# Two one-bank PSUM tiles in place of one two-bank tile, and a new hand-written order

## The chip, the cores and the metric

The kernel runs on one core of a Trainium2 chip. The time is device microseconds from launch to finish. TensorE does the matrix products, VectorE (DVE) and ScalarE (ACT) move and transform tiles, GpSimd (POOL) does a few memsets, and SyncE (SP) issues every DMA. Matrix products land in PSUM, which has eight banks of 128 partitions by 512 fp32 numbers.

## The reference, cut to what matters

```python
# x: 4 batches of 12480 tokens of 128 channels; inducing: 32 x 128
def mab(q, kv):
    a = softmax(q @ kv.T / sqrt(128))
    return a @ kv
h   = mab(inducing, x)          # 32 rows per batch, a sum over all tokens
y   = mab(x, h)                 # every token against the 32 rows
hid = y @ w_in                  # 128 -> 2048
out = (hid - tanh(hid)) @ w_out # 2048 -> 128
```

## The kernel before

**Tiling.** A batch of 12480 tokens is cut into seven slices of 1792 tokens (the last one overlaps its neighbour by 64). A slice of x, channels on partitions, is 896 KB (0.9175 MB) and takes one of 19 places called `big`; all 28 slices are loaded once. The pairs of slices (0,1), (2,3), (4,5) and (6) share one score tile each.

**First pass, for each batch b.** I call the steps by short names. `ldx s` loads slice s. `S1.s` (L275) makes the scores of a slice against the inducing rows, eight matmul records. `max1.g` (L299, DVE) moves the scores of pair g out of PSUM and takes a maximum. `spread1`, `fold1` (L313), `nb1` (L315) turn the maxima into one number. `exp1.g` (L324, ACT) and `tr1.g` (L326, DVE) give weights with tokens on partitions. The same slice is also needed with tokens on partitions: either `LDXN s` loads it a second time from a transposed copy in HBM, or `turn s.h` (L345, seven TensorE transposes for each half h) and `cpy s.h` (a copy of 128x896 by ACT, L168, or DVE, L170) make it. The set `LOADED` says which slices are loaded twice. `ACC s` (L357) adds the slice to the 32 sums over tokens in PSUM. `foldsum` (L365), `recip` (L369), `whole` (L375 or L377), `hT` (L379) and `cphT` end the batch's sum.

**Between the passes.** A small chain puts the 32 rows through the two weight matrices in linearised form: `up` (L275 with win_sb), `turned`, `tanh`, `series`, `tangent`, `column` (L435), `cpP1`, `points` (L441, L442), `cpP4`, `cpPm`, `away`, `far`. The weights arrive as 64-bit numbers and are put together as fp32 by DVE and ACT, five DVE steps and two ACT steps for each of eight blocks (L237 to L258).

**Second pass.** `S2.s`, `max2.g` (L478), `spread2`, `ones2` (L487), `nb2` (L490), `wg`, `exp2.g` (L500), then `L s` (L514): eight matmul records into two PSUM tiles, emptied by `ev s.0` and `ev s.1` (L530 on ACT or L532 on DVE), and `st s` stores the slice from its `big` place. The last two slices of the last batch are stored in halves, as soon as each half is emptied. A final chain (`bpe`, `bcopy`, `pick`, `least`, `bturn`, `gather`, `decide`) writes one flag that decides whether a general, slow path runs; with these inputs it does not.

**Order.** `ORDER` is a written list. Each word is the number of a step, the engine (P, A, D, S, G) and letters that choose places in the pools for its new tiles. Each engine runs its steps in this order, and so does SP: a DMA that waits holds up all DMAs behind it. Waits are made from the order: a step waits for those earlier in the list that touch the same tile, if one of them writes it.

**PSUM.** Three tiles `d` of two banks each take scores, transposes and outputs (six banks). One more tile of two banks, `side`, holds the rest: its first bank is the place `s` (the sums over tokens, `up`, `pick`, `bturn`), its second bank has three places `q` for all the small products. Two output halves, those in `SIDE`, batch 3 slice 0 half 1 and batch 3 slice 3 half 0, are written into the whole of `side` instead of a `d` tile.

Of the kernel before, what the change touches and what calls it, by code (L numbers as in the profile page):

```python
# [10 lines left out]
F32 = mybir.dt.float32  # L11
# [25 lines left out]
SIDE = frozenset(((3, 0, 1), (3, 3, 0),))  # L37
LOADED = frozenset(((0, 5), (1, 3), (1, 4), (1, 6), (2, 3), (2, 5), (2, 6), (3, 1), (3, 2), (3, 4), (3, 5), (3, 6),))
# [17 lines left out]
277Ac 372P 376Db 461Pgb 380A 278A 374P 473Sm 459P 301Pack 462D 381P 466Peb 302A 385Da 386Sd 390D 196S 464P 303A 292Pcas 293A 467D 383P 317A 471Phb
469P 294D 295S 472D 296Pacf 318A 298A 297D 327A 387P 304S 474Pcb 391Ab 475D 319Pacd 321D 482Pbl 392Pa 320A 299S 477D 483A 484Pa 393D 485A 323Pbcs
478Pa 154D 408Pda 322S 324A 325D 487Sk 407P 479D 409D 480A 197Pcba 326S 394Pa 410Pba 481Da 411P 395Db 198A 199A 396A 328Pbch 502Sj 412D 329A 486Pa
330A 398D 399Dc 436Pia 435P 437D 179Pcbr 476G 491Sf 489A 488P 500Sd 413Da 498A 506Si 504A 508D 400Pa 495Pak 181D 414Pc 415D 180A 509Pb 496A 490Da 397A
200S 493Pc 494A 401Aa 305Pabs 405Dc 182S 307D 510D 499Db 492P 402Pa 417A 306D 416A 403Aa 497P 404A 418Pbcf 501P 438Pha 331S 439D 505Da 426A 419A 503P  # L60
420A 427Pcbn 406D 440Dc 429D 507P 441Pa 511Ab 512Pb 428A 442D 431Pbar 513D 444A 432A 421S 514Pa 443A 527Pbc 433D 449Pbah 515Dc 453A 528P 451A 518D
529D 516A 519Db 517A 430S 450A 434S 530Pca 531P 308S 452S 581A 532D 454Pbco 456A 455A 525Da 520Pb 533Db 521Ac 457S 526D 445Pacq 446A 534Pa 535D 522Pb
524D 447A 448S 422Pbar 523Ac 555Pic 537A 582D 424D 423A 556P 557D 538Pahabac 542Pbcp 536A 546A 539A 540D 425S 541S 543D 558Pda 559D 580D 544A
551Pboaabc 583Ac 560Da 547Pacq 552A 553D 561Pa 562D 584Am 585Pa 564A 548A 549D 563A 565Pbcr 566D 586Aa 587Pa 574A 575Pabh 545S 567A 554S 550S 9Pc 578A
576A 588Da 589Pa 569Pbco 568S 570A 579S 577S 590D 571S 591D 7Pa 572D 573S 8Pa 5Pa
# [47 lines left out]
def fused_kernel(ctx, tc, xT, xn, indT, w_in, w_out, outT):  # L113
# [21 lines left out]
    pspool = ps_scope.__enter__()  # L135
# [36 lines left out]
    def place(tag):  # L172
        return Buf(lambda b: slots[tag][b.slot], tag)
# [7 lines left out]
    def fixed(t):  # L181
        return Buf(lambda b: t)
# [276 lines left out]
    def second(b, P4, Pm):  # L459
        def group(G):  # L460
# [34 lines left out]
            for g in G:  # L495
# [6 lines left out]
                def last(j, s):  # L502
                    ot, ds, outs, whole = place("big"), [], [], [[], []]
# [245 lines left out]
```

## Time and profile before

| | us |
|---|---|
| median of 3 runs | 178.69 |
| the three runs | 177.58, 178.69, 178.9 |
| the profiled execution | 177.38 |
| its span, first to last instruction | 175.6 |

The profiled execution is one run of its own; its span leaves out 1.78 us of its time. TensorE is busy for 149.2 us of the span, DVE for 126.7 and ACT for 110.8, and DMA packets fill 94.6% of the 16 DMA engines' time. No engine is busy all the time, so a busy share alone does not say which one sets the end. The table of stretches and the lists of waits do.

### The profile page before, as it was taken

How to read it: one execution, taken by the hardware profiler on the slowest of the kernel's cores; microseconds unless marked ns; L12 is line 12 of the kernel's file. 1: busy time of each engine (PE TensorE's matmuls, PEld its weight loads, DVE VectorE, ACT ScalarE, POOL GpSimd, SP SyncE). 2: the span in 40 equal slices, each digit the busy share in tenths (PEclk: the TensorE clock that was granted, in tenths of full speed). 3: DMA queues.
4: the chain of work that ended last, by engine and by line, in shares of the span. 5: the costliest groups of instructions: out<-in, count | busy, mean ns of one | idle time of the engine just before them, and what ended most of it. 6: DMA issues, size and time to landing. Idle time of an engine off the chain costs nothing.

```text
span 175.6 us, 4692 instructions
## 1 busy us (share of the span) xinstructions
PE 149.2 (85%) x1946; PEld 86.3 (49%) x1946; DVE 126.7 (72%) x290; ACT 110.8 (63%) x166; POOL 1.2 (1%) x10
## 2 busy tenths in 40 slices
PE   0779959999999899899977999999969898998900
PEld 0644628763376755535766545436656424434400
DVE  4285957899999949399782457698783798797810
ACT  2376419953568767485378456869737687999800
POOL 1000000000000000000000000000000000000000
PEclk9999999999999999999999999999999999999985
DMA  5999999999999999999999989999997698999991
GB/s 190 413 412 420 418 410 419 400 419 419 421 417 415 420 418 371 280 412 328 400 423 425 405 353 411 371 324 420 425 423 329 253 410 368 412 394 410 413 392 63
DMA packets 11405, 66.85 MB, mean 381 GB/s; under 512 B 1392, under 2 KB 1392, under 8 KB 11376
## 3 DMA queue, kind: packets, MB, share of 16 engines
q1 hardware_dynamic: 11376, 66.47, 94.6%
q8 instruction: 17, 0.28, 0.6%
q14 instruction: 12, 0.10, 0.2%
HBM read 40.91 MB, written 25.56 MB: 379 GB/s over the span
## 4 chain that ended last, share of the span: by engine, by line
PE 47%; DMA 19%; DVE 16%; ACT 9%; issue 4%; SPq 1%; ACTq 0%; DVEq 0%
PE d L275 12%; PE d L514 12%; PE side L357 10%; DMA big<-in_xT 9%; DMA big<-in_w_out 6%; PE d L345 5%; DMA big<-in_w_in 4%; DVE big L532 3%; ACT big L530 3%; ACT sl L324 2%; DVE sl L478 2%; PE side L435 2%; PE side L487 2%; DVE sl L299 2%; DVE et L326 1%
## 5 line engine op out<-in xcount | busy, mean ns | idle before, releaser
L530 ACT ACTIVATE big<-d,Pm,wg 128x896 f32<-128x896 f32 x35 | 37.4, 1093 | 14.1 <-PE d L514 11.2
L168 ACT COPY big<-d 128x896 f32<-128x896 f32 x29 | 25.6, 910 | 22.6 <-PE d L345 22.5
L345 PE MATMUL d<-ident,big 128*128 128x128 f32 x224 | 30.8, 285 | 7.6 <-DMA big<-in_xT 6.6
L345 PEld LDWEIGHTS d<-ident,big 128*128 128x128 f32 x224 | 25.9, 148 | 15.1 <-issue 7.2
L357 PE MATMUL side<-big,et 128*32 128x128 f32 x784 | 28.3, 275 | 3.4 <-DVE rs L369 1.4
L357 PEld LDWEIGHTS side<-big,et 128*32 128x32 f32 x784 | 23.1, 110 | 14.9 <-issue 6.2
L514 PE MATMUL d<-sl,k 32*128 32x448 f32 x216 | 29.6, 584 | 0.2
L275 PE MATMUL d<-big,indT_sb 128*32 128x448 f32 x224 | 27.1, 544 | 2.3 <-DMA big<-in_xT 2.1
L532 DVE TENSOR_SCALAR big<-d,wg,Pm 128x896 f32<-128x896 f32 x19 | 22.9, 1203 | 3.6 <-PE d L514 2.0
L275 PE MATMUL d<-big,hT 128*32 128x448 f32 x224 | 24.7, 543 | 0.5 <-ACT big L530 0.4
L299 DVE TENSOR_SCALAR_CACHE_REDUCE sl<-d 128x896 f32<-128x896 f32 (+1 forms) x16 | 15.5, 970 | 11.6 <-PE d L275 11.5
L478 DVE TENSOR_SCALAR_CACHE_REDUCE sl<-d 128x896 f32<-128x896 f32 (+1 forms) x16 | 15.4, 968 | 4.5 <-PE d L275 4.5
L500 ACT ACTIVATE sl<-sl,nbs 128x896 f32<-128x896 f32 (+1 forms) x16 | 15.2, 947 | 4.5 <-DVE nbs L490 4.5
L326 DVE STREAM_TRANSPOSE et<-sl 128x896 f32<-128x896 f32 (+1 forms) x16 | 15.7, 987 | 0.5 <-ACT sl L324 0.5
L514 PEld LDWEIGHTS d<-sl,k 32*128 32x128 f32 x216 | 9.8, 183 | 12.3 <-issue 4.8
L324 ACT ACTIVATE sl<-sl,nb 128x896 f32<-128x896 f32 (+1 forms) x16 | 15.0, 943 | 0.3 <-DVE nb L315 0.3
L275 PEld LDWEIGHTS d<-big,hT 128*32 128x32 f32 x224 | 7.0, 109 | 13.4 <-issue 7.9
L275 PEld LDWEIGHTS d<-big,indT_sb 128*32 128x32 f32 x224 | 7.5, 109 | 9.1 <-issue 5.0
L490 DVE TENSOR_REDUCE nbs<-side 128x1 f32<-128x128 f32 x8 | 2.3, 289 | 5.7 <-PE side L365 2.4
L244 ACT ACTIVATE big<-big 128x512 f32<-128x512 uint32 x8 | 5.6, 700 | 0.6 <-DMA big<-in_w_out 0.6
L251 DVE SCALAR_TENSOR_TENSOR big<-big 128x512 uint32<-128x512 uint32 x8 | 5.4, 686 | 0.5 <-ACT big L247 0.5
L247 ACT ACTIVATE big<-big,shift 128x512 uint32<-128x512 uint32 x8 | 5.5, 712 | 0.0
(115 smaller groups left out, 126.0 us busy)
## 6 DMA issues: line engine op xcount, KB each, us to landing
big<-in_xT SPq DMA_DIRECT2D x28, 896.0 KB, 11.2
outT<-big SPq DMA_DIRECT2D x23, 896.0 KB, 6.2
big<-in_xn SPq DMA_DIRECT2D x12, 896.0 KB, 12.3
outT<-big SPq DMA_DIRECT2D x3, 864.0 KB, 4.8
big<-in_w_in SPq DMA_DIRECT2D x4, 512.0 KB, 7.3
big<-in_w_out SPq DMA_DIRECT2D x4, 512.0 KB, 13.0
outT<-big SPq DMA_DIRECT2D x3, 448.0 KB, 6.3
outT<-big SPq DMA_DIRECT2D x1, 416.0 KB, 5.7
```

What stands on the lines that cost most here:

```text
L168: nc.scalar.copy(out=out, in_=in_)
L275: nc.tensor.matmul(ps[q * m:(q + 1) * m, :n], lhsT=w, rhs=row, start=True, stop=True)
L299: nc.vector.tensor_scalar(out=sl.get()[:, :n, :], in0=ps.get()[:, :n, :W], scalar1=1.0, scalar2=None, op0=ALU.mult, op1=ALU.max, accum_out ...
L324: nc.scalar.activation(out=t, in_=t, func=AF.Exp, scale=SC, bias=nb.get(), accum_out=sums.get()[:, g:g + 1])
L326: add("DVE", lambda e, et=et, sl=sl, n=len(pair): nc.vector.transpose(out=et.get()[:, :n * KB, :].rearrange("p k i -> p (k i)"), in_=sl.ge ...
L345: nc.tensor.transpose(out=o[:, k * 128:(k + 1) * 128], in_=x.get()[:, at:at + 128], identity=ident)
L357: nc.tensor.matmul(hacc.get()[q * m:(q + 1) * m, :C], lhsT=et.get()[:, j * KB + k, :], rhs=xn_t.get()[:, k * C:(k + 1) * C], start=at < NQ ...
L478: nc.vector.tensor_scalar(out=sl.get()[:, :n, :], in0=ps.get()[:, :n, :W], scalar1=1.0, scalar2=None, op0=ALU.mult, op1=ALU.max, accum_out ...
L500: nc.scalar.activation(out=t, in_=t, func=AF.Exp, scale=SC, bias=nb)
L514: nc.tensor.matmul(ds[q // 2].get()[:, q % 2, :W], lhsT=P4.get()[r, :], rhs=sl.get()[r, j, :], start=True, stop=True)
L530: nc.scalar.activation(out=dst, in_=src, func=AF.Identity, scale=wg.get(), bias=Pm.get())
L532: nc.vector.tensor_scalar(out=dst, in0=src, scalar1=wg.get(), scalar2=Pm.get(), op0=ALU.mult, op1=ALU.add)
```

## The change

The tile `side` becomes two tiles of one bank, `bank_s` and `bank_q`. The three `q` places stay in one bank together, at columns 0, 170 and 340. `SIDE` is gone, so all output halves use `d` tiles. `LOADED` has eleven slices in place of twelve, and others: batch 0 none (before: 5), batch 1 slices 3, 4 (before 3, 4, 6), batch 2 slices 1, 4, 5, 6 (before 3, 5, 6), batch 3 slices 0 to 4 (before 1, 2, 4, 5, 6). `ORDER` is new from the first word to the last.

```diff
-SIDE = frozenset(((3, 0, 1), (3, 3, 0),))
-LOADED = frozenset(((0, 5), (1, 3), (1, 4), (1, 6), (2, 3), (2, 5), (2, 6), (3, 1), (3, 2), (3, 4), (3, 5), (3, 6),))
+LOADED = frozenset(((1, 3), (1, 4), (2, 1), (2, 4), (2, 5), (2, 6), (3, 0), (3, 1), (3, 2), (3, 3), (3, 4),))
...
-    side = pspool.tile([128, 2, 512], F32, name="side")
     slots = {}
     for tag, n in PLACES.items():
         if tag in "sq":
-            slots[tag] = [side[:, 0, :]] if tag == "s" else [side[:, 1, k * 170:(k + 1) * 170] for k in range(n)]
+            bank = pspool.tile([128, 512], F32, name=f"bank_{tag}")
+            slots[tag] = [bank[:, k * 170:] for k in range(n)]
             continue
...
-                    ot, ds, outs, whole = place("big"), [], [], [[], []]
-                    for h in range(2):
-                        if (b, s, h) in SIDE:
-                            ds.append(fixed(side))
-                            whole[h] = [place(tag) for tag in "sqqq"]
-                        else:
-                            ds.append(place("d"))
+                    ot, ds, outs = place("big"), [place("d"), place("d")], []
...
-                    add("PE", pe, reads=[sl, part[g], P4], writes=ds, hold=[ot, *whole[0], *whole[1]])
+                    add("PE", pe, reads=[sl, part[g], P4], writes=ds, hold=[ot])
...
-                        add("ACT/DVE", ev, reads=[ds[h], ot, wg, Pm], writes=[done], hold=whole[h])
+                        add("ACT/DVE", ev, reads=[ds[h], ot, wg, Pm], writes=[done])
```

The two orders, with the numbers replaced by the names of the steps, for the parts that matter below (win and wout are the weight blocks):

```
SP, before, start: b0 ldx1, win3, win0, b0 ldx3, indT, win2, b0 ldx0, ldx2, ldx5, ldx4, ldx6, wout2, b1 ldx1, ...
SP, after,  start: b0 ldx2, wout3, b0 ldx1, indT, b0 ldx0, win3, b0 ldx3, ldx4, ldx5, ldx6, win2, win0, b1 ldx1, ...
SP, before, from the last load: b3 LDXN6, b0 st5, st3, b1 st6, b2 st0, st2, st3, b1 st3, b2 st5, st6, st4, st1,
    b3 st0, st1, st3, st2, st4, st6.1, st6.0, st5.0, st5.1
SP, after,  from the last load: b3 LDXN4, b0 st3, st4, st5, b1 st3, st2, b2 st2, st0, st5, st3, st4, st6, st1,
    b3 st0, st2, st3, st6.0, st6.1, st5.0, st5.1, st1, st4
stores ahead of the last load: 10 before, 9 after
TensorE, before: ... b3 foldsum, turn3.0, b1 L3, b3 ACC2, b2 points, b3 ACC3, b2 L0, b3 ACC4, ...
TensorE, before, the rest of the chain in batch 3: b3 ACC6, b2 ones2.2, b3 hT, b2 L3, b3 up, S2.0, b2 L5, b3 S2.1, S2.2, S2.3,
    b2 L6, b3 column, b2 L4, b3 ones2.0, points, b2 L1, b3 S2.4, S2.5, L0, L1, S2.6, L3, L2, ones2.2, bpe, L4, pick, L6, bturn, L5
TensorE, after, the same part: b3 ACC6, hT, b2 L3, b3 up, S2.0, b2 L5, b3 S2.1, S2.3, S2.2, b2 L4, b3 column, b2 L6,
    b3 points, ones2.0, b2 L1, b3 S2.4, S2.5, L0, S2.6, L2, ones2.2, L3, bpe, L6, pick, L5, bturn, L1, L4
DVE, before, after b0's first maximum: nb1, wout2 (2 steps), tr1.0; b3: recip, tr1.2, b1 ev3.0, b2 max2.3, b3 tr1.3
DVE, after,  after b0's first maximum: nb1, win2 (3 steps), tr1.0; b3: tr1.3, recip; end: least, gather, b3 ev1.0, decide, ev4.0
slices turned by TensorE in batches 0 to 3: 6, 4, 4, 2 before; 7, 5, 3, 2 after
128x896 copies: DVE 3 and ACT 29 before; DVE 8 and ACT 26 after.  Evictions: DVE 20 and ACT 36 before; DVE 19 and ACT 37 after
```

Six small matmuls (`idle0` to `idle5`, L220) keep TensorE going in gaps; both orders have them, in other places.

## Rows read from the trace of the kernel before

**Rows 1.** The page's head, busy time by engine, and DMA totals; the queue's share last.

```profile
span 175.6 us, 4692 instructions
PE 149.2 (85%) x1946; PEld 86.3 (49%) x1946; DVE 126.7 (72%) x290; ACT 110.8 (63%) x166; POOL 1.2 (1%) x10
...
DMA packets 11405, 66.85 MB, mean 381 GB/s; under 512 B 1392, under 2 KB 1392, under 8 KB 11376
...
q1 hardware_dynamic: 11376, 66.47, 94.6%
```

**Rows 2.** Busy us (and instructions) by engine in six stretches; clock, DMA share, GB/s last.

```profile
5.67:24.04 18.37, 15.24 (x114) 9.57 (x114) 13.20 (x23) 9.77 (x13) 0.00 (x0) 1.00 1.02 416
24.04:60.30 36.26, 34.57 (x526) 22.41 (x526) 32.91 (x77) 23.99 (x42) 0.24 (x2) 1.00 1.02 416
60.30:137.05 76.75, 71.69 (x1059) 42.50 (x1059) 53.21 (x114) 49.31 (x75) 0.24 (x2) 1.00 0.98 384
130.00:140.00 10.00, 9.19 (x160) 5.62 (x162) 5.13 (x11) 5.84 (x9) 0.00 (x0) 1.00 0.74 304
137.05:167.60 30.55, 27.71 (x251) 11.76 (x250) 25.45 (x63) 26.43 (x36) 0.00 (x0) 1.00 0.93 379
167.60:175.60 8.00, 0.00 (x0) 0.00 (x0) 0.00 (x0) 0.00 (x0) 0.00 (x0) 0.62 0.57 213
```

**Rows 3.** Timeline: the last first-batch load arrives; first sum over tokens (start, length, ...).

```profile
24.04 0.96 PE L275 MATMUL d<-big,indT_sb 128*32 128x448 f32 x8 [1.68 <-DMA big<-in_xT]
...
29.41 3.24 PE L357 MATMUL side<-big,et 128*32 128x128 f32 x112
```

**Rows 4.** Groups by line and form: count, busy us, mean ns, idle before and releasers.

```profile
L530 ACT ACTIVATE big<-d,Pm,wg 128x896 f32<-128x896 f32 x35 | 37.4, 1093 | 14.1 <-PE d L514 11.2 <-issue 1.1 <-ACT k L375 0.8
L345 PE MATMUL d<-ident,big 128*128 128x128 f32 x224 | 30.8, 285 | 7.6 <-DMA big<-in_xT 6.6 <-DVE sl L478 0.9
L357 PE MATMUL side<-big,et 128*32 128x128 f32 x784 | 28.3, 275 | 3.4 <-DVE rs L369 1.4 <-ACT k L168 1.4 <-DVE big L484 0.6
...
L168 ACT COPY big<-d 128x896 f32<-128x896 f32 x29 | 25.6, 910 | 22.6 <-PE d L345 22.5
...
L532 DVE TENSOR_SCALAR big<-d,wg,Pm 128x896 f32<-128x896 f32 x19 | 22.9, 1203 | 3.6 <-PE d L514 2.0 <-ACT wg L492 1.2 <-issue 0.4
...
L251 DVE SCALAR_TENSOR_TENSOR big<-big 128x512 uint32<-128x512 uint32 x8 | 5.4, 686 | 0.5 <-ACT big L247 0.5
...
L170 DVE COPY big<-d 128x896 f32<-128x896 f32 x3 | 3.3, 1086 | 0.0
```

**Rows 5.** TensorE's waits from 60.3 to 137 us: total, times, longest; first four of seven.

```profile
PE side L357 <- DVE rs L369: 1.4, 1, 1.4
PE side L357 <- ACT k L168: 1.4, 2, 1.0
PE d L345 <- DVE sl L478: 0.9, 1, 0.9
PE side L357 <- DVE big L484: 0.6, 1, 0.6
...
```

**Rows 6.** Timeline: two places where one half of the side tile waits for the other.

```profile
32.58 0.38 PE L365 MATMUL side<-sm,fold 128*128 128x1 f32 x2
...
32.89 1.07 PE L357 MATMUL side<-big,et 128*32 128x128 f32 x28
...
34.00 0.16 DVE L369 TENSOR_SCALAR rs<-side 128x1 f32<-128x1 f32 x1 [0.53 <-PE side L357]
...
128.46 0.15 DVE L369 TENSOR_SCALAR rs<-side 128x1 f32<-128x1 f32 x1
...
128.66 1.07 PE L357 MATMUL side<-big,et 128*32 128x128 f32 x28 [1.40 <-DVE rs L369]
```

**Rows 7.** Timeline: the end of the program.

```profile
164.62 1.03 PE L514 MATMUL d<-sl,k 32*128 32x448 f32 x8
...
166.37 1.21 DVE L532 TENSOR_SCALAR big<-d,wg,Pm 128x896 f32<-128x896 f32 x1
```

More of the change, by code (lines that the diff above doesn't have):

```diff
@@ L64 @@
[L64 to L65 removed]
+79Sa 1G 2D 3D 4Pa 66Sb 68D 76Sc 110Pad 112Pb 69A 103Pce 72D 111D 0S 74Sf 113D 104A 34Sg 105Pa 106D 37A 81Sh 77Pab 67D 100Pci 98Pa 99A 101D 70A 36D 75P
+78D 80Pbc 35D 84Sj 40D 86Sk 38A 82P 83D 117Pbl 71D 73D 124Pam 122Pc 118A 85Pcb 39D 123D 87P 125A 89Sn 127Pab 90Pdc 88D 41D 129Pb 91D 92G 26So 93D 128A
@@ new lines @@
+27D 94Pa 28D 29A 130A 95D 30A 115Pc 136Pbg 134Pa 32D 31D 96A 33D 10Sp 116A 211Sq 97Da 11D 108A 212Pec 18Sr 209Ss 109Db 12D 102Pa 120A 107P 19D 214So
+114P 13A 121Da 21A 210P 132A 16D 139D 20D 22A 119P 140Pa 216Si 133Db 213D 14A 24D 58Se 126P 131P 215Pdc 23D 135A 137A 50Sd 219Sl 138P 15D 141D 217P
+25D 17D 59D 142Aa 218D 60D 143Pa 144A 235Pbr 187Pca 186P 221Sm 158Pbc 236A 62A 51D 63D 159P 188D 54A 224Sb 52D 161Pab 160D 61A 64D 162P 222Pfa 220P
+42Sg 53A 189Pgc 163D 223D 190D 225Phb 226D 43D 227G 145Pa 245Pcn 56D 228D 45A 338Sp 55D 44D 46A 65D 340Sk 238Pbh 233Pa 246A 239A 229Pa 247Pc 234A 248A
@@ new lines @@
+258Pbe 259A 191Da 263Paa 230D 231A 192Pa 146Da 164Db 343Sj 256Pc 57D 345Sf 48D 232Db 47D 264A 240Pb 241A 149D 250Sc 254Sd 165Pb 49D 243A 265Pa 237Pa
+147A 341Peb 252A 348Sr 350Sg 244Da 242P 339P 257A 249P 344Pdc 166D 167A 177A 193D 150Db 342D 261A 251P 353Sh 168A 268D 253Da 151Pa 152Ab 262Db 266A
+346P 269Pa 153Pb 255P 349Pha 194A 155A 204A 463Sn 154Ab 347D 169Pcbd 260P 367Sc 351P 170D 171A 352D 148A 270D 205Pcbe 267P 206A 271Aa 207D 354Pga 355D
+272Pa 273D 178Pbca 195A 179D 287Pfa 288P 180A 291Pib 290P 289D 292D 173Paci 174A 274Pa 357D 175A 172S 315Pbb 293Da 208S 461Ss 356G 316P 358Pa 275Db
@@ new lines @@
+181S 468Sq 364Pcm 362Pa 466Sd 276A 176S 359D 317D 278D 360A 383Sl 294Pa 361Db 365A 363A 373Pbe 374A 385So 295D 378Pca 376Pa 371Pb 379D 369A 381A 277A
+318Pec 372A 471Sb 279Dc 377A 370Da 366Pa 280Pa 319D 368P 296A 281Da 464Pdc 387A 320Dc 321Pa 297A 391D 285Dc 286D 306A 473Sm 389Sc 392Pb 282Pc 196Pabi
+375P 197A 382Db 476Se 462P 469Pha 322D 380P 283Aa 198A 465D 284A 467P 388Da 302Pcba 470D 324A 384P 472Pga 303D 304A 393D 298Pcbl 323A 386P 300A 474P
+299D 325Pcbo 390P 475D 305S 327A 394Ac 326D 301S 477Pfa 328S 478D 480D 395Pb 329Pcbc 396A 481Pb 397Pa 411Pba 485Sa 330D 331A 482D 483A 410P 487Sk 489A
@@ new lines @@
+200Pcbl 398Dc 412D 202A 414Pca 413P 332S 484Da 201A 333A 479G 401D 399A 400A 495A 415D 402Db 439Pdb 491Sp 504A 438P 493So 334Pacg 335A 486Pa 336A 337S
+416Dc 497Sa 403Pb 440D 488P 496Db 404Ad 182Pbar 501Pcc 184A 405Pb 417Pc 490Da 502D 183A 156Db 506Pak 157D 307Pbcj 507A 418D 185S 492P 308D 441Pha 309A
+494P 511D 199S 442D 443Dc 311Pbch 429A 406Ad 444Pc 408Db 512Pa 420A 313A 312D 409D 499Pa 407D 421Pbcg 419A 423D 445D 203S 500A 498P 508Pa 503P 422A
+509D 430Pcbr 447A 505Db 446A 510P 5Pa 513D 514Ac 432D 515Pa 431D 434Pabk 435A 516D 517Pa 530Pcc 436D 452Pbal 456A 531P 454A 534Pfa 314S 533P 518Db
@@ new lines @@
+521D 519A 532D 453A 522Dc 448Pbcq 535D 520A 528Da 584A 310S 450A 433S 449A 523Pa 524Dc 536Da 457Pacr 424S 459A 525Pa 529D 537Pc 458A 538D 425Pbcg 540A
+427A 526Da 539A 558Pha 527A 585D 426D 549A 559P 541Pbcb 542A 560D 587Am 455S 543D 437S 561Pba 562D 563Dd 451S 550Pbck 586Ae 564Pa 8Pa 551D 460S 552A
+565D 566A 577A 554Pabr 556A 588Pa 555D 567A 583D 578Pcbq 428S 544S 589Dd 579A 590Pa 591Dd 553S 557S 581A 580S 572Pacb 592Pa 593D 582S 573A 574S 575A
+545Pbak 546D 576S 594D 547A 568Pcae 548S 6Pb 7Pb 9Pb 569D 570A 571S
```

20 lines of the change are left out of this document (removed).

## The prediction

> **What bounds the kernel now.** I read the page's busy shares and DMA totals first. The queue's packets fill 94.6% of the DMA engines and TensorE is busy for 85% [rows 1], so either may set the end, and the table of stretches has to decide [rows 2]. Its columns show: up to 24 us the DMA stream is full (share 1.02) and TensorE idles 3.1 of 18.4 us; batch 0's last slice arrives at 24.04, after a wait for the load [rows 3]. From 24 to 60 us TensorE (34.6 of 36.3) and DVE (32.9) are both nearly full. From 60.3 to 137 us TensorE is the bound: busy 71.69 of 76.75, while DVE and ACT have over 23 us free each. DMA is full too (0.98), but no row of TensorE's waits there names a load. At 137 batch 3's last ACC ends; then the last second passes run, with evictions, TensorE and stores all at 0.8 to 0.93, and the stores end the program. The DMA share dips to 0.74 from 130 to 140: stores stand in the queue waiting for evictions, so even DMA is late there because compute is late.
>
> So the end follows the time at which b3 ACC6 ends, plus 38.55 us of tail (175.6 less 137.05). What can be won ahead of it is TensorE's idle time, 5.06 us in the stretch from 60.3. The groups by form show where it lies: ACC alone has 3.4 us of idle time before it, with releasers recip (L369), cpP4 (L168) and spread2 (L484) [rows 4]; the list of TensorE's waits has the same three and four smaller ones [rows 5]. The timeline shows what kind of wait this is [rows 6]. At 34.00 `recip` starts when an ACC ends, though the `foldsum` that it reads began at 32.58 and lasted 0.38. At 128.66 an ACC starts 0.05 us after `recip` has read (128.46 plus 0.15). `recip` reads the second bank of `side`, ACC writes the first: they share no number. The two banks are waited for as one tile.
>
> **The change part by part.**
>
> *Two tiles.* The waits of ACC for readers of the other bank go: 3.4 us of TensorE idle, three of them the ends of queues on DVE and ACT (1.4, 1.0 and 0.6), one 0.4. This is safe to book only for the old order; the new one may queue other things. What stays is waiting inside one bank; the rows show it as small, since the waits that don't stand before ACC are 0.9 us or less each [rows 5]. The Trainium skill, "PSUM — Partial Sum Buffer", section "PSUM bank collisions raise a hardware error", says to guard PSUM by bank and quadrant, not by address; by it the three `q` places, still in one bank, go on excluding each other, and the 1.7 us that are left of the stretch's idle time (5.06 less 3.4) would stay whatever the order does, so that the term worked out next would be -1.9 in place of -3.2.
>
> *New order on TensorE.* On the two written orders I counted, between batch 0's first ACC and batch 3's last, the places where a TensorE step needs a result that DVE or ACT makes from an earlier TensorE step, with less TensorE work between than that move takes. Before there are ten (b3 ACC3 right behind b2 points is one), after there are two. The waits that such places gave before are what is left of the 5.06 us after the three queued ones (3.0), 2.1 us; two in ten leave 0.4. New queued waits I cannot see in a list; bounds are 0 and the 3.0 that the old order had, I take the middle, 1.5. So 5.06 becomes 1.9: **-3.2 us** (bounds -4.7 and -1.7).
>
> *LOADED, twelve to eleven.* One transfer of 0.9175 MB less is 2.2 us of DMA at the 416 GB/s of the first two stretches [rows 2]. One store fewer also stands ahead of the last load, so 1.8 MB (4.4 us) less must pass before it. That cancels no TensorE wait, since none for a load is there; it makes room for the 3.2 us, which DMA would otherwise have to deliver faster at a share of 0.98. I book 0 and check it as a rival. In exchange 14 transposes are added: 224 take 30.8 us, so 1.9 us [rows 4]. By batch it is +14 in b0, +14 in b1, -14 in b2. Those of b0 lie ahead of the first ACC, under 3.1 us of idle TensorE [rows 2]; if that cover is gone they cost 1.9. b1 and b2 cancel by 137 us. Net 0 (0 to +1.9).
>
> *Copies and evictions.* DVE gets five copies of 1.086 us more and one eviction of 1.203 fewer, +4.2 us; ACT -3 x 0.910 + 1.093, -1.6 [rows 4]. Three of the five copies are in batch 0 ahead of its maximum, where DVE has 18.37 - 13.20 = 5.2 us free [rows 2]; without that cover they cost 3.3. Two fall after 60 us, where DVE has 23.5 us free. In the full stretch from 24 to 60 the DVE work from `nb1` of b0 to `tr1.0` of b1, summed by the same rows over both orders, is 0.9 us longer in the new one. I take **+0.5** (0 to +2.4, the upper end if nothing of the copies ahead is absorbed).
>
> *Start.* Two weight blocks instead of three are loaded ahead of batch 0's last slice: 0.524 MB at 416 GB/s is 1.3 us earlier at 24.04. But the new order puts three weight steps (0.686 each, L251 the nearest row) between `nb1` and `tr1.0` on DVE, the old one two lighter ones, 0.7 to 1.3 us later. First ACC at 29.41 as before [rows 3]: 0 (-0.6 to +0.7). SP meets nothing else on the way: all these loads go to empty places. POOL's memset stays behind `max1.3`.
>
> *Tail.* Behind b3 ACC6 both orders have the same TensorE steps but for one `ones2` and one idle matmul: twelve slices of the second pass and the closing chain. The last eviction before started at 166.37, 0.7 us after its matmul ended, held up by the small steps of `decide` on DVE [rows 7]; the new order has `decide` ahead of its last DVE eviction too. New is that the last two stores are whole slices, not halves: 0.46 MB at 379 GB/s [rows 2] is 1.2 us more after the last eviction, if the queue has run empty by then. The share of 0.93 says that it mostly has not. The two halves that used `side` now need a `d` tile, an eviction's 1.2 us each at worst. Only two of 56 evictions used the extra place, so that the loss ends there. The Trainium skill, "Perfetto Trace Analysis", section "Matmul Optimizations", asks for all eight banks to be used for parallelism; by it giving up a fourth place for output is a loss, up to the 2.4 us of those two evictions; no row here shows what the place was worth. I take **+0.5** (0 to +2.4).
>
> Sum: -3.2 + 0 + 0 + 0.5 + 0 + 0.5 = -2.2 us. The profiled execution, 177.38 (span 175.6 and 1.78 around it), would become 175.2. It lies 1.31 below the median of the runs; the same difference on the median 178.69 gives **176.5**.
>
> **Rivals.**
>
> *A. New waits take the place of the old.* Queued waits of 3.0 us come back elsewhere and the small costs stay: -1.7 + 1.0 at the middle, and up to 0.5 more for transposes, so -0.7 to 0: about 178.3. For it: three waits of the old order were ends of queues, and any order has queues. Against it: eight of ten tight places are gone. That the split does nothing at all ends here too: it would if the waits were kept by bank already, but rows 6 show otherwise.
>
> *B. DVE in the weight stage (slower).* DVE is busy 32.9 of 36.3 us between 24 and 60, and what is left of the 40 weight steps on DVE and 16 on ACT must pass there before `column` of b0. If the copies ahead of it are not absorbed, b1's first ACC comes 2.4 us later, and everything behind it on TensorE with it; if queued waits return as well, 178.69 + 2.4 = 181.1. It decides once more than the 5.2 us of free DVE time ahead of 24 us is needed. For: +3.3 us of copies there. Against: the cover is larger than that, and x arrives earlier.
>
> *C. The room on DMA is used.* No queued waits arise (-4.7), and with 1.8 MB less ahead of the last load the dip of 130 to 140 (0.26 of 10 us) closes by a third, 0.9; with +0.5 for the tail -4.7 + 0.5 - 0.9 = -5.1: 173.6. Against: the stores still wait for evictions.
>
> *D. DMA is the bound all the way.* Then only the bytes count: -2.2 us, 176.5 as well, by another way. It does not change the sum, but the waits would then name loads.
>
> **How the numbers follow.** Forecast (with D) 0.48, A 0.25, B 0.15, C 0.12. The forecast's own range, by the bounds of its terms, is 174.5 to 178.2. About 1% (1.8 us, so 176.9 and 180.5) is what measurements of this kernel can tell from no change; the three runs spread by 0.7%. The forecast holds 0.39 faster and 0.09 same; A is same but for 0.02 slower; B is slower; C is faster. Faster 0.51, same 0.32, slower 0.17. The range must leave out no more than 2 in 10: from 173.6, which takes half of C, to 180.2, which takes A and the lower part of B.
>
> **What the profile after would show.** The list of waits should have no ACC waiting for `recip`, cpP4 or nb2 and no `recip` waiting for an ACC; TensorE's idle time from b1's ACCs to b3 ACC6 should be about 2 us, not 5. b3 ACC6 should end near 134.5, and the last load land some 4 us earlier than before. DVE should be busy about 131 us, TensorE about 151, DMA bytes 65.93 MB. The first ACC should start at 29 to 30, b1's first no later than 1 us after before. The tail should still be about 39 us. The prediction is wrong if b1's first ACC is over 2 us late (B), if new releasers such as an eviction or a copy stand before ACC with 3 us (A), or if the tail is over 40.5 us, because the last whole stores start late.

## The result, and the profile after

The changed kernel takes 173.24 us (median of four runs, 172.59 to 173.93); the kernel before, beside it, takes 178.16 (177.58 to 178.9). The ratio is 0.9722, with a 95% interval of 0.9659 to 0.9786: faster, by more than forecast, 0.4 us below the low end of the range. Some executions of a kernel fall into a slower state: the medians of the variants below leave these out, and of the profiles only that of `new_b2_load2` (182.29 us) is of one. The profiled execution of the changed kernel is its slowest run, 173.93, with a span of 172.1. Against the profiled execution before (177.38, span 175.6) that is 3.45 us less.

The page's head, busy time by engine and DMA totals:

```profile
span 172.1 us, 4717 instructions
...
PE 151.3 (88%) x1960; PEld 88.9 (52%) x1960; DVE 131.3 (76%) x296; ACT 108.9 (63%) x162; POOL 1.4 (1%) x10
...
DMA packets 11262, 65.94 MB, mean 383 GB/s; under 512 B 1376, under 2 KB 1376, under 8 KB 11232
...
q1 hardware_dynamic: 11232, 65.56, 96.0%
```

TensorE and DVE have more work than before [rows 1] and the kernel is still shorter. Most of the gain is time in which TensorE waited. The table of stretches says where, with the same columns as [rows 2]; its third row is cut where batch 3's last ACC ends, now at 133.11 in place of 137.05:

```profile
24.00:60.30 36.30, 33.72 (x502) 23.89 (x502) 33.01 (x77) 25.95 (x43) 0.46 (x2) 1.00 0.99 385
60.30:133.11 72.81, 71.03 (x1092) 41.48 (x1081) 57.43 (x122) 49.56 (x78) 0.24 (x2) 1.00 1.00 396
133.11:164.00 30.89, 29.10 (x250) 12.30 (x250) 25.44 (x64) 24.91 (x32) 0.00 (x0) 1.00 1.01 412
164.00:172.10 8.10, 0.00 (x0) 0.00 (x0) 0.00 (x0) 0.00 (x0) 0.00 (x0) 0.72 0.53 203
...
130.00:140.00 10.00, 9.62 (x122) 4.12 (x124) 8.99 (x19) 5.17 (x9) 0.00 (x0) 1.00 1.01 422
...
29.47:133.11 103.64, 99.98 (x1549) 61.86 (x1544) 85.51 (x186) 70.64 (x114) 0.57 (x3) 1.00 1.00 392
```

From 60.3 us to b3 ACC6 TensorE idles 72.81 - 71.03 = 1.78 us; before it was 5.06 [rows 2]. The last row is the whole way from the first ACC to b3 ACC6, 3.66 us idle. The same way before, from 29.41 to 137.05, took 4.00 us longer: idle time was 6.37, so 2.71 of the 4.00 are idle time, and the other 1.29 are busy time.

```profile
29.41:137.05 107.64, 101.27 (x1547) 61.65 (x1539) 82.94 (x182) 69.89 (x111) 0.35 (x3) 1.00 0.99 393
```

The dip of the DMA share between 130 and 140 us (0.74) is gone (1.01). What lies behind b3 ACC6 takes 38.99 us, before 38.55. TensorE's waits in the stretch from 60.3 to 133.2 are these, all that the list has:

```profile
PE d L274 <- DMA big<-in_xT: 0.7, 1, 0.7
PE d L274 <- DVE big L169: 0.6, 1, 0.6
PE d L274 <- DVE sl L477: 0.3, 1, 0.3
PE d L507 <- DVE big L525: 0.2, 1, 0.2
```

None stands before an ACC, and none names a small product; compare [rows 5]. The groups by form, the same as in [rows 4]:

```profile
L523 ACT ACTIVATE big<-d,Pm,wg 128x896 f32<-128x896 f32 x37 | 39.6, 1096 | 22.0 <-PE d L507 18.2 <-issue 3.1 <-ACT sl L323 0.4
...
L344 PE MATMUL d<-ident,big 128*128 128x128 f32 x238 | 31.7, 287 | 2.2 <-DMA big<-in_xT 2.0
L356 PE MATMUL bank_s<-big,et 128*32 128x128 f32 x784 | 28.6, 274 | 0.0
...
L525 DVE TENSOR_SCALAR big<-d,wg,Pm 128x896 f32<-128x896 f32 x19 | 22.9, 1208 | 6.6 <-PE d L507 3.6 <-issue 2.4 <-ACT big L523 0.4
...
L169 DVE COPY big<-d 128x896 f32<-128x896 f32 x8 | 8.6, 1090 | 3.8 <-PE d L344 2.3 <-DMA outT<-big 1.0 <-issue 0.5
```

The idle time in front of ACC, 3.4 us before, is 0.0. Last, the timeline: the last load of batch 0, the first ACC, the one large wait of b1's weight stage, the last batch's foldsum, ACCs and recip, and the last eviction, for [rows 3, 6, 7]:

```profile
23.39 0.96 PE L274 MATMUL d<-big,indT_sb 128*32 128x448 f32 x8 [1.50 <-DMA big<-in_xT]
...
29.47 2.46 PE L356 MATMUL bank_s<-big,et 128*32 128x128 f32 x82
...
45.45 1.71 PE L274 MATMUL d<-big,indT_sb 128*32 128x448 f32 x16 [1.74 <-DVE sl L477]
...
125.93 0.28 PE L364 MATMUL bank_q<-sm,fold 128*128 128x1 f32 x2
...
128.17 1.07 PE L356 MATMUL bank_s<-big,et 128*32 128x128 f32 x28
...
130.08 1.07 PE L356 MATMUL bank_s<-big,et 128*32 128x128 f32 x28
...
131.81 0.12 DVE L368 TENSOR_SCALAR rs<-bank_q 128x1 f32<-128x1 f32 x1
...
162.17 1.21 DVE L525 TENSOR_SCALAR big<-d,wg,Pm 128x896 f32<-128x896 f32 x1
```

In [rows 6] an ACC waited 1.40 us for recip. Here recip reads its place 5.6 us after foldsum was done, at the end of DVE's queue, and two ACCs run meanwhile without waiting. `recip` comes no sooner than it did; no ACC stands behind it any more.

### The profile page after: what moved, and what is told of

Read it like the earlier page. It is cut to its first block, busy times and chain, and to the rows that moved or that the text cites. A ratio compares the mean times of both kernels' runs of the same rounds, so it can differ in the third digit from the quotient of the medians.

```text
span 172.1 us, 4717 instructions
## 1 busy us (share of the span) xinstructions
PE 151.3 (88%) x1960; PEld 88.9 (52%) x1960; DVE 131.3 (76%) x296; ACT 108.9 (63%) x162; POOL 1.4 (1%) x10
## 4 chain that ended last, share of the span: by engine, by line
PE 50%; DMA 25%; ACT 9%; DVE 8%; issue 3%; SPq 0%; DVEq 0%; ACTq 0%
DMA big<-in_xT 16%; PE d L274 15%; PE d L507 12%; PE bank_s L356 11%; DMA outT<-big 6%; ACT big L167 4%; DMA big<-in_w_out 3%; DVE sl L477 3%; PE d L344 3%; PE bank_q L434 2%; ACT big L523 2%; PE d L219 1%; ACT sl L323 1%; PE bank_s L274 1%; ACT big L246 1%
## 5 line engine op out<-in xcount | busy, mean ns | idle before, releaser
L523 ACT ACTIVATE big<-d,Pm,wg 128x896 f32<-128x896 f32 x37 | 39.6, 1096 | 22.0 <-PE d L507 18.2
L344 PE MATMUL d<-ident,big 128*128 128x128 f32 x238 | 31.7, 287 | 2.2 <-DMA big<-in_xT 2.0
L507 PE MATMUL d<-sl,k 32*128 32x448 f32 x224 | 32.0, 585 | 0.6 <-ACT big L523 0.4
L344 PEld LDWEIGHTS d<-ident,big 128*128 128x128 f32 x238 | 28.0, 149 | 8.3 <-issue 4.8
L356 PEld LDWEIGHTS bank_s<-big,et 128*32 128x32 f32 x784 | 23.7, 110 | 10.0 <-issue 5.9
L356 PE MATMUL bank_s<-big,et 128*32 128x128 f32 x784 | 28.6, 274 | 0.0
L167 ACT COPY big<-d 128x896 f32<-128x896 f32 x26 | 22.7, 908 | 7.4 <-PE d L344 7.4
L507 PEld LDWEIGHTS d<-sl,k 32*128 32x128 f32 x224 | 10.9, 183 | 14.0 <-issue 3.9
L169 DVE COPY big<-d 128x896 f32<-128x896 f32 x8 | 8.6, 1090 | 3.8 <-PE d L344 2.3
L219 PE MATMUL d<-fold,ones 128*128 128x256 f32 x12 | 4.1, 452 | 3.0 <-DVE fold L214 3.0
```

The costliest lines, as they stand in the source:

```text
L167: nc.scalar.copy(out=out, in_=in_)
L344: nc.tensor.transpose(out=o[:, k * 128:(k + 1) * 128], in_=x.get()[:, at:at + 128], identity=ident)
L356: nc.tensor.matmul(hacc.get()[q * m:(q + 1) * m, :C], lhsT=et.get()[:, j * KB + k, :], rhs=xn_t.get()[:, k * C:(k + 1) * C], start=at < NQ ...
L507: nc.tensor.matmul(ds[q // 2].get()[:, q % 2, :W], lhsT=P4.get()[r, :], rhs=sl.get()[r, j, :], start=True, stop=True)
L523: nc.scalar.activation(out=dst, in_=src, func=AF.Identity, scale=wg.get(), bias=Pm.get())
```

## The experiments

The theory after the result is this: the split of the tile is the gain, because the old tile made TensorE wait for readers of the other bank, and what b3 ACC6 gains the end gains. The rivals: the new order is the gain (fewer places where TensorE needs a fresh result); the 0.92 MB less DMA is the gain; TensorE is no longer the bound and something else is. The runs were timed in four groups, each with its own runs of the kernel before, whose medians are 177.17, 177.09, 177.19 and 177.36 us. "The end of b3 ACC6" below is from each run's profile.

### The old order without and with the split

`old_noside` is the kernel before with all outputs in `d` tiles, the tile still joined. Batch 3's L1 and L2 stand a few words later in the order, because only three places are left. `old_split` is the same with two tiles.

```diff
-SIDE = frozenset(((3, 0, 1), (3, 3, 0),))
 # ORDER, batch 3: L0 538Pahabac -> 538Pabh, L3 551Pboaabc -> 551Pcbo
 #   L1 (542Pbcp) behind 540D, L2 (547Pacq) behind 552A
 # old_split alone:
-    side = pspool.tile([128, 2, 512], F32, name="side")
...
+            bank = pspool.tile([128, 512], F32, name=f"bank_{tag}")
+            slots[tag] = [bank[:, k * 170:] for k in range(n)]
```

> The same kernel as the one with the split, but the two banks stay one tile: only the two output halves move to d tiles. Theory P: the waits of ACC stay at 3.4 us; the tail loses a place, 0 to +1.5 us against the kernel before. Theory D: 0, the tail is full of stores. The difference to the kernel with the split is what the split alone gives to the old order: 2.5 to 3.5 us by P, under 1 by D.

> The old order and the old twelve second loads, with the two-bank tile split into two one-bank tiles; the two output halves that used it take d tiles, and for that two steps (L1 and L2 of batch 3) stand a little later in the list. Theory P (TensorE's waits of ACC for readers of the other bank are on the path): TensorE's idle before ACC, 3.4 us, goes, b3 ACC6 ends near 133.7 in place of 137.05, and the time is 2.5 to 3.5 us below the kernel before. Theory D (the DMA stream sets the end, and the new order gains by its fewer bytes and by keeping the stream full): the waits go, but the time moves by less than 1 us, since the bytes are the same and the queue holds the same steps. Theory O (order alone): no gain, under 0.5 us.

Measured: `old_noside` 179.35 us, ratio to the kernel before 1.012 [1.0064, 1.0176]; `old_split` 174.81, 0.9853 [0.9801, 0.9906]. The split alone gives 4.5 us, where 2.5 to 3.5 was expected. b3 ACC6 ends at 136.98 without and at 133.05 with it. The group of ACC in the first kernel, then in the second:

```profile
L356 PE MATMUL side<-big,et 128*32 128x128 f32 x784 | 28.3, 275 | 3.9 <-DVE rs L368 1.4 <-ACT k L167 1.4 <-DVE big L483 0.6
```

```profile
L356 PE MATMUL bank_s<-big,et 128*32 128x128 f32 x784 | 28.3, 275 | 0.3 <-DVE et L325 0.3
```

Two more things follow. `old_noside` is 2.2 us slower than the kernel before with b3 ACC6 where it was: that is what the fourth place for output, with the two steps that had to move, was worth in the old order. In `old_split` it shows in TensorE's list of waits behind b3 ACC6, as two waits of L for evictions:

```profile
PE d L507 <- DVE big L525: 1.4, 1, 1.4
PE d L507 <- ACT big L523: 0.8, 2, 0.4
```

And `old_split`, with all ten tight places of the old order, has its b3 ACC6 at about the time of the new kernel: 133.05, and 133.10 and 134.02 in two profiles of the same order and split further down, against 131.14 to 133.11 in four profiles of the new order.

### The new order without the split

```diff
+    side = pspool.tile([128, 2, 512], F32, name="side")
...
-            bank = pspool.tile([128, 512], F32, name=f"bank_{tag}")
-            slots[tag] = [bank[:, k * 170:] for k in range(n)]
+            slots[tag] = [side[:, 0, :]] if tag == "s" else [side[:, 1, k * 170:(k + 1) * 170] for k in range(n)]
```

> The new order and the new eleven second loads, with both banks in one tile again. Theory P: waits between the banks come back, about as many as the old order had (3 to 4 us of TensorE idle before ACC), and the time is 2 to 4 us above the new kernel. Theory D: under 1 us above it, since the bytes and the queue are the same. Theory O: the new order was made with few round trips, so that the tile matters little: under 0.5 us.

Measured: 178.47 us, 1.007 [1.0042, 1.0097]; b3 ACC6 ends at 136.93. The new order and its eleven loads, in one tile, are 1.3 us slower than the kernel before. But they also have one output place fewer. Against `old_noside` (179.35), which has the same three places, they are 0.9 us faster; in two tiles, against `old_split`, the ratios of the new kernel further down (0.9787, 0.9766) are 1.2 to 1.5 us better. So the order is worth about one microsecond, and the place that it gives up costs as much or more. TensorE's waits from the first ACC to b3 ACC6, the first three:

```profile
PE side L356 <- DVE nbs L489: 2.0, 2, 1.6
PE side L356 <- DVE et L325: 1.0, 1, 1.0
PE side L434 <- DVE m L425: 0.6, 1, 0.6
```

The new order has queued waits of its own: ACC waits for `nb2` (L489), which reads the other bank at the end of DVE's queue. In the changed kernel that wait isn't there because the tile is split, not because of the order.

### Undoing four waits by listing alone

`old_flip` is the kernel before, joined tile and all. Four ACCs are only listed ahead of the reader that they waited for; each engine's own sequence stays as it was, so what turns round is who waits for whom.

```diff
 # ORDER, the words around each moved step
-148Pa 149Da ... 190D 246P 201A
+148Pa 246P 149Da ... 190D 201A              # b1 ACC2 ahead of b0 cpP1
-291A 277Ac 372P 376Db
+291A 372P 277Ac 376Db                       # b2 ACC2 ahead of b1 cpP4
-307D 510D 499Db 492P 402Pa
+307D 492P 510D 499Db 402Pa                  # b3 ACC2 ahead of b3 recip
-416A 403Aa 497P 404A
+416A 497P 403Aa 404A                        # b3 ACC3 ahead of b2 cpP4
```

> The old kernel with its two-bank tile, its second loads and its order on every engine; only four ACC steps (b1 ACC2, b2 ACC2, b3 ACC2, b3 ACC3) are listed ahead of the read in the other bank that each of them waited for, so that the reader waits for the ACC in place of the ACC for the reader. Theory P (TensorE waiting at these four places is the price of the joined tile): TensorE's 3.4 us of idle before ACC go, and the time falls by 2 to 3.5 us without any split. Theory Q (waits between the banks cost more than what stands in that row, in many places and on DVE and ACT too): they reappear elsewhere, under 1.5 us of gain.

Measured: 175.35 us, 0.9898 [0.9865, 0.993]. That is 1.8 us, between what the two theories named; the split with the same four output places gives 3.9 (`old_split_side`, next). Where the rest lies is read by setting the starts of TensorE's steps in the kernel before beside those of `old_flip` and of `old_split`. A step that starts earlier by more than the one ahead of it has lost a wait. Three stretches of `old_flip`'s TensorE, then the same of `old_split`:

```profile
72.09 0.39 PE L313 MATMUL side<-mq,fold 128*128 128x4 f32 x2 [0.46 <-DVE k L377]
...
93.62 0.92 PE L275 MATMUL d<-big,indT_sb 128*32 128x448 f32 x6
95.07 0.96 PE L357 MATMUL side<-big,et 128*32 128x128 f32 x26 [0.53 <-ACT Pm L168]
...
129.66 1.03 PE L514 MATMUL d<-sl,k 32*128 32x448 f32 x8 [0.36 <-ACT Pm L168]
```

```profile
71.58 0.39 PE L312 MATMUL bank_q<-mq,fold 128*128 128x4 f32 x2
...
93.11 0.92 PE L274 MATMUL d<-big,indT_sb 128*32 128x448 f32 x6
93.68 1.04 PE L356 MATMUL bank_s<-big,et 128*32 128x128 f32 x28
...
127.61 1.03 PE L507 MATMUL d<-sl,k 32*128 32x448 f32 x8
```

Against the kernel before, `old_flip`'s shifts are -0.80 at b1 ACC2, -1.11 at b2 ACC2, then +0.90 at 95.07, -1.21 at b3 ACC2, +0.40, -0.43 at b3 ACC3 and +0.44 at 129.66: -1.8. With the split they are -0.81, -0.52 at 71.58, -1.11, -1.47, +0.46 (`points` waits 0.40 for recip, both in `bank_q`) and -0.43: -3.9. In the joined tile a listing only chooses who waits: with the ACC ahead, the next reader (cpPm, L168) waits for the ACC, and the next TensorE step waits for that reader. `fold1`, which needs a small place, waits 0.46 us for `whole`, which reads the sums. Two tiles end all of these at once.

### The old order with the split and its four output places

`old_split_side` is the kernel before, its order unchanged to the letter. The two halves of `SIDE` are written into the two bank tiles, 448 columns each, and emptied by two instructions of 128x448 each.

```diff
-                            ds.append(fixed(side))
+                            ds.append(None)
...
+                            to = banks["sq"[q % 2]] if ds[q // 2] is None else ds[q // 2].get()[:, q % 2, :]
+                            nc.tensor.matmul(to[:, :W], lhsT=P4.get()[r, :], rhs=sl.get()[r, j, :], start=True, stop=True)
...
+                            parts = [(dst, d.get()[:, :, :W])] if d else [(dst[:, i, :], banks["sq"[i]][:, :W]) for i in range(2)]
```

> The old order and second loads with the tile split, but the two output halves go on using both banks: each is emptied by two operations of 128x448, one for each bank. The split alone gave 4.5 us to the old order where the two halves take d tiles, and giving up the place cost 2.2. Theory P with the loss of the place as a cost of its own: 173 us (the old kernel's 177.1 less 3.9 for b3 ACC6, plus 0.2 for two operations in place of one), level with the new kernel. If the place is worth nothing once the tile is split: 174.8, as the old order with the halves in d tiles.

Measured: 173.25 us, 0.9754 [0.9703, 0.9804]. It was run again beside the new kernel, unchanged:

> The old order with the split tile, its twelve loads and its four output places, timed once more beside the new kernel on one chip. If the split alone is the gain: the same as the new kernel of the next run within 0.7 us, near 0.976 of before. If the new order and the eleven loads are worth something besides: it is slower than the new kernel by 1 us or more.

> The new kernel unchanged, on the same chip as the old order with the split tile. If the split alone is the gain: 173.2 to 174 us and no difference to that run over 0.7 us. If the new order is worth something besides: faster than it by 1 us or more.

173.07 us (0.9737 [0.9693, 0.978]) and 173.44 (0.9766 [0.9714, 0.9819]), against 177.36 before: no difference that these runs can tell. The group of ACC in `old_split_side`, whose b3 ACC6 ends at 133.10:

```profile
L358 PE MATMUL bank_s<-big,et 128*32 128x128 f32 x784 | 28.3, 275 | 0.2 <-DVE et L327 0.2
```

The whole gain is to be had by splitting the tile and cutting two evictions in half, without a new order and without fewer loads.

### Bytes and TensorE work in the new kernel

`new_again` is the new kernel unchanged, timed in one group with `new_store_less` and `new_pe_more`. `new_12` loads batch 0 slice 5 a second time, behind the load of weight block win1, in place of its turns. `new_store_less` leaves out the store of batch 0 slice 5, so that slice's output is not written. `new_tail_less` leaves out the store of batch 2 slice 1, one of the last fourteen slices stored. `new_pe_more` puts five matmuls of 128x256 (about 2.2 us) ahead of batch 3's S1.4.

```diff
 # new_12
+LOADED with (0, 5);  ORDER: without turn 5.0, cpy 5.0, turn 5.1, cpy 5.1 of b0, with 127Sb behind win1's load
 # new_store_less; new_tail_less has (2, 1)
-                        add("SP", lambda e: nc.sync.dma_start(...),
+                        add("SP", lambda e: (b, s) != (0, 5) and nc.sync.dma_start(...),
 # new_pe_more
+        for _ in range(5):
+            nc.tensor.matmul(more.get()[:, 0, :256], lhsT=ones, rhs=fc, start=True, stop=True)
```

> The new kernel with a twelfth second load: batch 0 slice 5 is loaded (behind the block win1) and not turned, so 14 transposes and two ACT copies go and 0.9175 MB comes to the stream. Theory D: the stream is full from 10 us to the end, so +2.2 us (0.9175 MB at 416 GB/s) above the new kernel. Theory P: the stream has room, and TensorE has 1.9 us less to do in a stage where it waits for loads anyway: -1 to +0.5 us.

> The new kernel once more, as the base for the other kernels of this call: 172.6 to 173.9 us by both theories.

> The new kernel without the store of batch 0 slice 5, the third step of the SP queue behind the last load (that slice of the output is not written). Theory D (from 118 us on the DMA stream is full, and its bytes set the end): 0.9175 MB less at 412 GB/s is 2.2 us less than the new kernel. Theory P (TensorE and the evictions behind it set the end, and the stream only keeps up): under 0.5 us less.

> The new kernel with five more matmuls of 128x256 (some 2.2 us of TensorE work that nobody reads) ahead of S1.4 of batch 3, between the first and the last ACC. Theory P: everything behind comes later, +1.8 to +2.2 us. Theory D: the stream has 16 transfers to go when b3 ACC6 ends, TensorE's delay hides behind them: 0 to +0.7 us.

> The new kernel without the store of batch 2 slice 1, one of the last fourteen slices' worth of stores, which are issued after b3 ACC6 (that slice of the output is not written). Leaving out a store ahead of them moved the time by under 0.5 us. Theory T (behind b3 ACC6 the stores set the end: 14 slices at 412 GB/s are 31 us): 1.8 to 2.2 us less than the new kernel's 173.5. Theory E (the evictions set the end there too): under 0.6 us less.

| run | us | ratio to before, 95% | b3 ACC6 ends |
|---|---|---|---|
| new_12 | 173.45 | 0.9778 [0.9713, 0.9844] | 133.32 |
| new_again | 173.29 | 0.9787 [0.9724, 0.9851] | 132.23 |
| new_store_less | 172.55 | 0.9766 [0.9693, 0.9839] | 131.92 |
| new_pe_more | 174.09 | 0.9823 [0.9771, 0.9874] | 133.73 |
| new_tail_less | 174.01 | 0.9742 [0.9653, 0.9832] | 134.1 |

0.92 MB more or less is 2.2 us of a full stream. Against `new_again` it moves the ratio by 0.001 and 0.002, which is 0.2 and 0.4 us (and both times to the fast side), while the intervals reach 1.2 to 1.3 us to either side. So 2.2 us more in `new_12` is ruled out, 2.2 us less in `new_store_less` only just. In `new_store_less` the stream simply dips again; the table of stretches of that run:

```profile
130.00:140.00 10.00, 9.61 (x100) 3.53 (x104) 9.21 (x22) 4.77 (x9) 0.00 (x0) 1.00 0.84 343
```

`new_tail_less` is inconclusive: the three runs counted are at 171.9, 174.01 and 174.39, and nothing was gained that can be told. 2.2 us more of TensorE work move b3 ACC6 by 1.5 us against `new_again` in the profiles, which is within the spread of the unchanged kernel's own (131.14 to 133.11), and the median by 0.8 us, with intervals that overlap. Part of it fills the wait of 0.7 us for a load that stands at 103 to 105 us in the new kernel's profiles and is missing from that run's. So neither resource is shown to be the bound alone now.

### A load in place of a turn, at two places

Batch 2 slice 3 is loaded twice in place of being turned. In `new_b2_loaded` the load stands behind that of slice 1; its `big` place had not been left by batch 0's slice 2, so that part of the output is overwritten. In `new_b2_load2` it stands behind that slice's store.

```diff
+LOADED with (2, 3);  ORDER: without turn 3 and cpy 3 of b2
+  new_b2_loaded: 367Sc 376Sa      (behind b2 LDXN1)
+  new_b2_load2:  181S 376Sa       (behind b0 st2)
```

> The new kernel with batch 2 slice 3 loaded a second time, behind the load of batch 2 slice 1, in place of 14 transposes and two copies between the first and the last ACC: 1.7 to 1.9 us less for TensorE, 0.9175 MB (2.2 us) more for the stream. Theory P: -1 to -1.9 us. Theory D: +1.5 to +2.2 us. If both are near their limits, 0 to +2.2, and the load's place in the queue decides.

> The new kernel with batch 2 slice 3 loaded a second time behind the store of batch 0 slice 2 (about 75 us), where its place is free, in place of 14 transposes and two copies. Before, this load had been put into a place that another slice still needed, so that run told nothing of the trade. Theory P: TensorE has 1.7 us less ahead of b3 ACC6: -0.8 to -1.7 us against 173.5. Theory D (a load of batch 3 is already waited for by 0.7 to 1.2 us): the 2.2 us of stream make that wait longer, 0 to +1.5 us.

Measured: 179.0 us, 1.0112 [1.0055, 1.0169], and 178.6, 1.0065 [1.0015, 1.0115]. Both lose all that the split had won, 5 us and more, for the 0.92 MB that cost `new_12` nothing that could be told; no theory had expected that. In `new_b2_loaded` TensorE has one wait that the new kernel doesn't have, 5.9 us for a load:

```profile
PE bank_s L356 <- DMA big<-in_xn: 5.9, 1, 5.9
```

As its place was wrongly chosen, that run tells little more than that a load can come to stand before ACC at all. In `new_b2_load2` a reason can be read. Its profiled execution took 182.29 us, so only the kind of wait is taken from it, not what it costs. SP's waits for a store ahead of a load of the transposed copy (in total, times, longest), the stretches from 80 to 110 us, and TensorE's step at the end of the gap:

```profile
SPq L334 <- DMA outT<-big: 11.6, 3, 9.9
```

```profile
80.00:90.00 10.00, 8.74 (x148) 6.45 (x148) 8.77 (x25) 8.64 (x16) 0.00 (x0) 1.00 0.50 167
90.00:100.00 10.00, 2.41 (x44) 1.18 (x44) 1.66 (x3) 1.78 (x3) 0.00 (x0) 0.84 0.99 367
100.00:110.00 10.00, 9.95 (x140) 4.92 (x132) 4.08 (x7) 3.84 (x6) 0.00 (x0) 0.82 1.02 422
```

```profile
99.37 1.72 PE L274 MATMUL d<-big,indT_sb 128*32 128x448 f32 x8 [7.59 <-ACT big L523]
```

The load stands directly behind the store that empties its place. It waits 9.9 us until that store has landed, and every DMA behind it in SP's queue waits too, so the stream falls to half. From 91.8 us on TensorE stands idle for 7.6 us. Its granted clock, 1.00 before, falls in this gap and is at its lower level, 0.50 or 1.2 GHz, from 97 to 103 us (means of 0.84 and 0.82 in the last two stretches): eight matmul records that take 0.96 us elsewhere take 1.72. In `new_b2_loaded` too the clock falls, to a mean of 0.66 from 70 to 80 us, with the wait of 5.9 us. So a long wait for a load costs TensorE more than the wait. The bytes are those of `new_12`; the slice and its place in the queue are what differ, and that the place is what costs is read from this one profile.

### The last stores in halves

The new kernel leaves 162.17 + 1.21 = 163.38 to 172.1, 8.72 us, behind its last eviction; before it was 175.6 less 167.58, 8.02 [rows 7]. `new_halves` stores the two slices that come last in halves.

```diff
-                        if b == B - 1 and s >= NS - 2:
+                        if b == B - 1 and s in (1, 4):
 # ORDER: st5 and st6 whole; st1.0 behind decide, st4.0 behind ev4.0
```

> The new kernel, with the two stores that come last, those of slices 1 and 4 of batch 3, cut in halves, each stored when its half is emptied, in place of those of slices 5 and 6, which the old order had last. If the 0.7 us that lie more between the last eviction and the end than in the kernel before come from whole stores at the end: the end lies 8.0 us behind the last eviction in place of 8.7, and the time is 0.5 to 1 us less than the new kernel's. If two evictions that run side by side leave nothing to gain, or the end is set otherwise: within 0.3 us of the new kernel.

Measured: 172.96 us, 0.9737 [0.9695, 0.9779], 0.5 under `new_third` beside it, which the intervals can't tell from nothing. The profile speaks against the reason. Its stretches from b3 ACC6 to the last eviction, and from there to the end:

```profile
131.14:161.40 30.26, 28.81 (x250) 12.30 (x250) 25.42 (x64) 24.90 (x32) 0.00 (x0) 1.00 1.00 414
161.40:171.00 9.60, 0.28 (x2) 0.00 (x0) 0.00 (x1) 0.00 (x0) 0.00 (x0) 0.71 0.54 204
```

The end lies 9.60 us behind the last eviction, not 8.0, with the same stream at 1.00 ahead of it. In this run b3 ACC6 ended 1.6 us earlier than in `new_third`, whose order is the same up to there, and the end only 0.6: the queue of stores was still full. In `old_split_side_2` the stretch ahead of the last eviction has a share of 0.95, and 8.04 us are left:

```profile
134.02:164.36 30.34, 27.87 (x250) 11.76 (x250) 25.61 (x64) 26.66 (x37) 0.00 (x0) 1.00 0.95 389
164.36:172.40 8.04, 0.00 (x0) 0.00 (x0) 0.00 (x1) 0.00 (x0) 0.00 (x0) 0.62 0.56 211
```

So the whole last stores are not shown to cost anything; the new kernel's last stores wait in a stream that is full.

## Why the prediction was too long

The direction and the mechanism (an ACC waits for a reader of the other bank) were right, the size was not. The step that failed is the term for the two tiles and the order, -3.2, which took TensorE's busy time as unchanged; and the base was off. The forecast was 3.26 us too long, and that splits into three parts: the sum gave 175.2 for the profiled execution, which was 173.93 (1.27); 1.31 was added to go from the profiled execution to the median; and the profiled execution after is itself 0.69 above its median. The forecast's own range, 174.5 to 178.2, doesn't come out of the bounds of its terms: as they stand they add up to -5.3 and +5.7, which is 173.4 to 184.4, and the measured 173.24 lies just below that too.

**The bound.** Right for the kernel before and loose for the new one, whose end follows b3 ACC6 only in part (last section). The end lies 38.3 to 39.0 us behind b3 ACC6 in the profiles before and after and in nine of the runs, 39.6 to 39.9 in three others (`new_joined`, `new_halves`, `new_b2_loaded`), 39.3 in `new_b2_load2`, and 40.2 and 40.5 in the old order with three places.

**Two tiles and new order, -3.2.** The step that failed, and in three ways. First, the sum counted idle time alone and put the change of TensorE's busy time at nothing, without a reason. From the first ACC to b3 ACC6 idle time fell by 2.71 us (6.37 to 3.66; -3.2 + 0.5 was forecast), but the busy time of the same steps fell as well, by 101.27 - 99.98 = 1.29. This is the first part above, 1.27. The split has a share in it: three profiles of joined kernels in the old order have 101.2 to 101.3 us in that stretch, three of split kernels in that order 100.8; in the new order the joined kernel has 102.0 and four profiles of the new order in two tiles 99.9 to 100.6. Why the same steps are busy for less, and how much of it belongs to the single run, is open; the profile models the ends of matmuls, so its line between idle and busy time is not exact.

Second, the cause was put into two parts, the split and eight tight places fewer. The runs show that the split gives 4.5 us on the old order and about 5 on the new one (`new_joined` against `new_again` and `new_third`), while the new order gives about one, which the lost output place takes back: the old order with the split and its four places is level with the new kernel. Third, 1.5 us were booked for new queued waits. The order does have such waits, `new_joined` shows them, but in two tiles they don't reach TensorE. 1.78 us of idle time are left where 1.9 was forecast; that number came out right by luck, since what waits remain are for loads, copies and score tiles.

From the Trainium skill's rule on guarding PSUM by bank ("PSUM — Partial Sum Buffer", section "PSUM bank collisions raise a hardware error") the prediction worked out that 1.7 us of waits among the `q` places would stay whatever the order does. In `old_split` the list does show four waits in `bank_q`, 0.5 and three of 0.4: 1.7. In the new kernel none is left, so "whatever the order does" was wrong. No run here tests the rule itself, since the three places share a tile of the program as well as a bank.

**LOADED, 0.** Right: eleven or twelve loads make no difference (`new_12`, and `old_split_side` with twelve). The sign that was named with it failed: the last load was to land some 4 us earlier, but it was issued at 118.08, and before no later than 117.70.

**Copies and evictions, +0.5.** Right in kind: b1's first ACC starts at 57.45, before at 56.34, and on the way there TensorE has one large wait, 1.74 us for DVE at 45.45, in the weight stage. 1.1 later is a little more than the "no later than 1 us" that was named.

**Start, 0.** Right: the load is there at 23.39, before at 24.04, and the first ACC starts at 29.47, before at 29.41.

**Tail, +0.5.** Right in size (38.99 less 38.55), not in reason: whole stores at the end are not shown to cost. The fourth output place, for which the prediction named up to 2.4 us from the evictions' length, is worth 2.2 in the old order (`old_noside`). The Trainium skill's "Perfetto Trace Analysis", section "Matmul Optimizations", asks for all eight PSUM banks to be used; both kernels do use all eight, so the runs price a place for output, not a bank. In the new order L waits 0.4 us for evictions there, not 2.2; that order was not run with a fourth place.

**The base, +1.31.** Wrong. The three runs before had a median of 178.69; 50 later runs have medians of 177.1 to 177.4, and the profiled execution, 177.38, stood for them better than the three did. With its counterpart after, 0.69, it is six tenths of the 3.26 us. Beside the later bases the unchanged new kernel gains 3.8 and 3.9 us (0.9787 and 0.9766), not the 4.9 of the first comparison.

**The rivals.** A (new waits) did not come, though its waits exist in the order: it would have been true of the new order in one tile. B (DVE) came with 1.1 us and not 2.4. C gave the nearest time (173.6), by luck: the dip of 130 to 140 does close, but the 0.92 MB less gain nothing, and idle time from 60.3 us on fell by 3.3 us, not 4.7. D is out: the old bytes with the split give the same time.

## What to carry to other kernels

When the list of waits shows an engine waiting for a reader of data that it doesn't touch, look at which tile both name: here a tile of two banks was waited for as one, and splitting it can be worth more than the waits that the list names (3.4 us listed ahead of ACC, 3.9 to 4.5 won on the old order). Reordering inside the joined tile only chose who waits. Before crediting a new order, run the structural edit alone on the old one, with everything else that the old one has; here that gave the whole gain.

## What was not expected of the hardware

A DMA stream at 96% of its time was neither the bound nor free: 0.92 MB more in an empty place changed nothing that could be told (0.9778 against 0.9787), the same 0.92 MB queued right behind the store that empties its place cost about 5 us (178.6 against 173.3 to 173.4). And b3 ACC6 of one and the same program up to there ended between 131.14 and 133.11 us in four profiles, while the spans lay between 171.0 and 172.1: the full stream behind it takes up part of such differences.
